# Sixty-feature groups for kv and M in a gated attention and MLP kernel, with M's last rows sent through HBM

## The chip, the cores and the metric

The kernel runs on one core of a Trainium2 chip. The time is device microseconds of one execution. The five engines are TensorE (PE, with its weight loads PEld), VectorE (DVE), ScalarE (ACT), GpSimd (POOL) and SyncE (SP, here a queue that only issues DMAs).

## What is computed

Two branches on the same 2048 tokens of 640 features, mixed by a gate. Branch A is linear attention with 32 heads of 20 features, branch B an MLP with token shifts.

```python
# A, H = 32 heads, Dh = 20
pq, pk = phi(q), phi(k)                      # phi(t) = where(t>0, t+1, exp(t)) + 1e-6
kv  = einsum("bhsd,bhse->bhde", pk, v)       # 20x20 for each head
z   = einsum("bhsd->bhd", pk)
num = einsum("bhqd,bhde->bhqe", pq, kv)
den = einsum("bhqd,bhd->bhq", pq, z)[..., None] + 1e-6
a   = (num / den) @ wo
# B
h   = gelu(layernorm(x) @ w1)                # its four quarters shifted by +1, -1, +2, -2 tokens
x1  = x + shifted(h) @ w2
b   = x1 + gelu(layernorm(x1) @ w3) @ w4
out = g * a + (1 - g) * b                    # g = sigmoid(sum(x * gate_w))
```

## The kernel before

Everything is kept in SBUF in bf16 and summed in PSUM, which has eight banks of 512 fp32 columns. The work comes in this order: q and k of each of 16 token tiles (128 tokens), with phi on ACT and DVE; G = x^T pk, gathered over the tokens in PSUM (`gr_step`, `gt_step`); then w1 and w2 of branch B, w3, and a long stretch in which `a_tile` and `w4_tile` alternate for the 16 token tiles and write the output. Because v = x wv, kv is computed from G: kv = wv^T G.

The part around the change:

- `kvt_group` (L950, its matmuls L964) makes the transposed kv in blocks of 120 features (six heads; R6 = 120). For each of six blocks, the last of 40, five matmuls with a 128x128 weight tile. The first call does four blocks, the second two.
- `lt_evac` (L968) multiplies each block by a mask that keeps the 20x20 diagonal pieces and writes it as `Lt`, on DVE (L643).
- `m_group(r)` (L981) multiplies a block of `Lt` by the matching rows of wo (`wo_aug`): M = kv wo, one matmul of 512 columns and one of 128 (L613), evacuated on ACT (L669). Blocks 0 to 4 go to rows 0 to 119 of `M_sb[:, r, :]`. Block 5 has the last 40 features, which go to `Mt`.
- `m_tail` (L991) copies the 40 rows of `Mt` by five DMAs, eight rows each, to rows 120 to 127 of the five tiles of `M_sb`, so that M lies in five full tiles of 128 rows.
- `qn_scale` (L1065) divides phi(q) by the denominator and writes it in the same order of features, a main part (L1077) and a tail; `qt_tile` (L1080) transposes it by a DMA on SP into `pqnT`.
- `a_tile` (L1085) multiplies `pqnT` by `M_sb`; its first matmuls are the first to read `M_sb`.

Other lines: L613 is the helper of nearly all matmul groups; L1050 is `w3_half`, which uses the array as two halves of 64 columns; L1115 and L1118 are `w4_half`, which uses it as two halves of 64 rows; L1136 is w4; L669 and L668 are ACT operations; L635, L643, L650 and L652 are elementwise operations on DVE or POOL; L286 is any DMA copy, L282 any DMA transpose.

Order. Each piece of work is an item with a stream, a duration and dependencies (`IT.add`). A planner (`_Items.run`) picks, item by item, the one that can start first by its own cost figures, and so fixes at build time the order of instructions on each engine. At run time every engine, the SP queue too, goes through its list strictly in order and waits on semaphores. PSUM banks are chosen by the planner as well: `bank()` and `pair()` take the bank, or the aligned pair, that comes free first, and a bank in `bank_hold` is not given away.

Before, SP's list around the change is: transposes of `xn` up to number 7, five copies of `m_tail`, transposes 8 to 11, the first six transposes of q, transposes 12 to 15, then q's other transposes.

Of the kernel before, what the change touches and what calls it, by code (L numbers as in the profile page):

```python
# [19 lines left out]
EPS_LN = 1e-5  # L20
EPS_PHI = 1e-6
NK = D + 4
R6 = 120

SB_LO = 16512
SB_HI = 229344
# [403 lines left out]
def _build(nc, A_x, A_wqkv, A_wo, B_w1, B_w2, B_w3, B_w4, gate_w, out, dbg=None, stop=None):  # L430
# [47 lines left out]

    ones_c = pa.alloc("ones_c", [128, 768], BF16)
    ident = pa.alloc("ident", [128, 128], BF16)  # L480
    mask = pa.alloc("mask120", [128, 6, 20], BF16)
    mask_t = pa.alloc("mask_t", [128, 6, 20], BF16)
# [188 lines left out]
    def memset(engf, ap, val):  # L671
        return engf(lambda e: e.memset(ap, val), [], [ap])
# [54 lines left out]
    def load_wvo():  # L727
        dp = [k_done[11]]
        sch.dma("pool", wv[:, :, :], A_wqkv[:, 2 * D:3 * D].rearrange("(k p) f -> p k f", p=128), "wv", deps=dp)
        for r in range(6):  # L730
            n = min(R6, D - R6 * r)
            sch.dma("pool", wo_aug[0:n, r, :], A_wo[R6 * r:R6 * r + n, :], "wo", group_total=6, deps=dp)

    memset(pool, ones_c[:], 1.0)
    aselect(ident[:], ones_c[:, 0:128], [[-1, 128]], ALU.is_equal, 0, 1)
    memset(pool, negh[:], -0.5)
    aselect(mask_t[0:120], ones_c[0:120, 0:120].rearrange("p (b d) -> p b d", b=6), [[-20, 6], [0, 20]], ALU.is_ge, 0, 1)
    aselect(mask[0:120], mask_t[0:120], [[20, 6], [0, 20]], ALU.is_ge, 19, -1)
# [209 lines left out]
    kv_bank = {}  # L948

    def kvt_group(h):  # L950
        b = pair()
        kv_bank[h] = b
        bank_hold.update((b, b + 1))
        mms = []
        for q_, r in enumerate(range(4) if h == 0 else range(4, 6)):
            n = min(R6, D - R6 * r)
            for k in range(KD):
                mms.append((ps[:, b, R6 * q_:R6 * q_ + n], wvf[:, D * k + R6 * r:D * k + R6 * r + 128], GT[:, k, R6 * r:R6 * r + n],
                            q_ == 0 and k == 0, k == KD - 1))

        def fn(e):
            ins = None
            for o, l, r_, st_, sp_ in mms:
                ins = e.matmul(o, l, r_, start=st_, stop=sp_, skip_group_check=True)  # L964
            return ins
        pe(fn, [wvf[:, :], GT[:, :, :]], [ps[:, b, 0:480], ps[:, b + 1, 0:1]], cost=len(mms) * 60.0)

    def lt_evac(h):  # L968
        b = kv_bank[h]
        for q_, r in enumerate(range(4) if h == 0 else range(4, 6)):  # L970
            n = min(R6, D - R6 * r)
            src = ps[0:n, b, R6 * q_:R6 * q_ + n].rearrange("p (h m i) -> p h m i", m=5, i=4)
            msk = mask[0:n, 0:n // DH, :].rearrange("p h (m i) -> p h m i", i=4)
            if r < 5:
                dst = Lt[0:n, r, 0:n].rearrange("p (h m i) -> p h m i", m=5, i=4)
            else:
                dst = Lt[0:n, r, 0:n].rearrange("p (m h i) -> p h m i", m=5, i=4)
            tt(dve, dst, src, msk, ALU.mult)
        bank_hold.difference_update((b, b + 1))

    def m_group(r):  # L981
        n = min(R6, D - R6 * r)
        kr = R6 if r < 5 else 128
        b = pair()
        mm_group(ps[:, b, 0:512], [(Lt[0:kr, r, :], wo_aug[0:kr, r, 0:512])])
        mm_group(ps[:, b + 1, 0:128], [(Lt[0:kr, r, :], wo_aug[0:kr, r, 512:D])])
        src = psf[0:n, 512 * b:512 * b + D]
        dst = M_sb[0:n, r, :] if r < 5 else Mt[0:n, :]
        activation(dst, src, ACTF.Copy)

    def m_tail():  # L991
# [9 lines left out]
    for h in range(2):  # L1001
        IT.add("KVF", ("kvt", h), 0.0, lambda h=h: kvt_group(h), deps=[(("g", KD - 1), 1.0), (("gr",), 2.5)])
        IT.add("KVF", ("lt", h), 0.0, lambda h=h: lt_evac(h), deps=[(("kvt", h), 0.0)])
# [61 lines left out]
    def qn_scale(t):  # L1065
        sd = qn_slot[t]
        ts(dve, dnr[:, 0, sd, :], dnr[:, 0, sd, :], EPS_PHI, None, ALU.add, ALU.bypass)
        dve(lambda e: e.reciprocal(dnr[:, 1, sd, :], dnr[:, 0, sd, :]), [dnr[:, 0, sd, :]], [dnr[:, 1, sd, :]], cost=350.0)
        blk = pq_tok[:, t, :].rearrange("p (j c) -> p j c", c=128)
        main = (blk[:, :, 0:R6].rearrange("p j (a d) -> p j a d", d=DH),  # L1070
                pq_tok[:, t + 1, 0:5 * R6].rearrange("p (j a d) -> p j a d", a=6, d=DH),
                dnr[:, 1, sd, 0:30].rearrange("p (j a) -> p j a", a=6).unsqueeze(3).to_broadcast([128, 5, 6, DH]), 850.0)
        tail = (blk[:, :, R6:128].rearrange("p m (h i) -> p h m i", i=4),
                pq_tok[:, t + 1, 5 * R6:D].rearrange("p (h m i) -> p h m i", h=2, i=4),
                dnr[:, 1, sd, 30:32].unsqueeze(2).unsqueeze(3).to_broadcast([128, 2, 5, 4]), 150.0)
# [218 lines left out]
```

## Time and profile before

| | |
|---|---|
| median of 3 runs | 263.45 us (263.12 to 265.74) |
| the profiled execution, whole time | 262.97 us |
| its span | 260.9 us |
| busy: PE, PEld, DVE, ACT, POOL | 257.1, 133.0, 149.1, 107.2, 97.3 us |
| share of PE in the chain that ended last | 97% |
| matmuls of kvt (L964) | 30, start 77.0 to 79.5 us |
| matmuls of `m_group` | 12, start 114.7 to 137.6 us |
| copies of `m_tail` on SP | 5, start 118.3 to 121.3 us |
| first matmul that reads `M_sb` | 139.8 us |

A matmul's duration in the profile counts its whole way through the array, and matmuls overlap; so the time that a group takes is read from the start of its first matmul to the start of the next group's. A view of one engine's timeline gives start, length, engine, line, operation and count, and in brackets how long the engine had been idle and what released it. In the rows of groups stand the busy time, the mean of one in ns, and the idle time before them.

### The profile page before, as it was taken

What the parts mean: (1) busy time and instruction counts of PE and PEld (TensorE: products, weight loads), DVE (VectorE), ACT (ScalarE), POOL (GpSimd) and SP (SyncE); (2) the same over time, 40 slices, a digit from 0 to 9 for tenths busy, and PEclk for the clock granted to TensorE, in tenths of its full rate; (3) what the DMA queues carried; (4) which work ended last, traced back from release to release, by engine and by line L of the source; (5) the groups of instructions that cost most, each with busy time, mean ns of one, the idle gap of its engine ahead of it and who ended that gap; (6) DMA issues with size and microseconds to landing.
All of it is one profiled execution on the core that took longest, in us unless ns stands there. A gap on an engine that the chain in (4) does not pass through costs nothing.

```text
span 260.9 us, 4205 instructions
## 1 busy us (share of the span) xinstructions
PE 257.1 (99%) x1651; PEld 133.0 (51%) x1651; DVE 149.1 (57%) x267; ACT 107.2 (41%) x216; POOL 97.3 (37%) x150
## 2 busy tenths in 40 slices
PE   8999999999999999999999999999999999999996
PEld 3555555544455555555444545554455544455553
DVE  2497887899903799979993407991033410143333
ACT  1396677751365757674974240005500045100000
POOL 5013995859964017958763202320011200011000
PEclk9999999999999999999999999999999999999999
DMA  7755999652766991363585610232000020000211
GB/s 205 247 90 139 171 206 156 172 108 50 102 126 126 333 353 36 71 78 59 102 125 111 122 25 0 47 92 65 0 3 0 0 103 0 0 3 0 101 53 50
DMA packets 51283, 24.98 MB, mean 96 GB/s; under 512 B 42644, under 2 KB 49853, under 8 KB 51264
## 3 DMA queue, kind: packets, MB, share of 16 engines
q1 hardware_dynamic: 49824, 21.15, 36.8%
q0 software_dynamic: 1152, 3.28, 5.4%
q8 instruction: 13, 0.21, 0.3%
q10 hardware_dynamic: 288, 0.30, 0.3%
q14 instruction: 6, 0.05, 0.1%
HBM read 12.04 MB, written 2.62 MB: 56 GB/s over the span
## 4 chain that ended last, share of the span: by engine, by line
PE 97%; DMA 1%; DVE 1%; issue 0%
PE ps L613 61%; PE ps L1136 21%; PE ps L811 7%; PE ps L887 2%; PE ps L791 1%; DMA x_tok<-in_A_x_dram 1%; PE ps L1050 1%; PE ps L1118 1%; DVE x_tok L652 1%; PE ps L964 1%; PE ps L888 1%; PE ps L624 0%; PE ps L792 0%; DVE xT L678 0%; PE ps L1115 0%
## 5 line engine op out<-in xcount | busy, mean ns | idle before, releaser
L613 PE MATMUL ps<-xnT,w 128*128 128x512 bf16 x360 | 82.3, 379 | 0.0
L1136 PE MATMUL ps<-w,h2T 128*128 128x512 bf16 (+1 forms) x416 | 58.8, 299 | 0.0
L669 ACT ACTIVATE h2T<-ps 128x512 bf16<-128x512 f32 x52 | 30.4, 598 | 66.5 <-PE ps L613 66.5
L613 PEld LDWEIGHTS ps<-xnT,w 128*128 128x128 bf16 x360 | 34.0, 98 | 37.4 <-issue 0.4
L652 DVE SCALAR_TENSOR_TENSOR x_tok<-ps,stg,abx 128x512 bf16<-128x512 f32 (+1 forms) x32 | 17.2, 550 | 61.6 <-PE ps L1136 61.6
L635 POOL TENSOR_SCALAR abx<-x_tok,stg 128x640 f32<-128x640 bf16 x16 | 14.8, 928 | 99.6 <-DVE x_tok L652 95.1
L1136 PEld LDWEIGHTS ps<-w,h2T 128*128 128x128 bf16 x416 | 32.4, 98 | 25.6 <-issue 1.1
L635 POOL TENSOR_SCALAR xn<-x_tok,st 128x640 bf16<-128x640 bf16 x32 | 38.9, 1222 | 14.5 <-DMA xnT<-xn 14.0
L669 ACT ACTIVATE Er<-ps 128x640 bf16<-128x640 f32 x32 | 22.4, 706 | 18.1 <-PE ps L613 8.5
L668 ACT ACTIVATE junk<-x_tok 128x640 bf16<-128x640 bf16 x32 | 23.6, 738 | 3.7 <-DVE x_tok L650 3.2
L669 ACT ACTIVATE hsT<-ps 128x512 bf16<-128x512 f32 (+1 forms) x32 | 18.9, 594 | 14.7 <-PE ps L613 14.3
L613 PE MATMUL ps<-M_sb,pqnT 128*128 128x512 bf16 (+1 forms) x160 | 24.3, 299 | 0.0
L613 PE MATMUL ps<-w,hsT 128*128 128x512 bf16 (+1 forms) x160 | 23.9, 299 | 0.0
L652 DVE SCALAR_TENSOR_TENSOR abx<-ps,stg,abx 128x640 f32<-128x640 f32 x16 | 14.1, 884 | 15.8 <-PE ps L613 15.8
L613 PE MATMUL ps<-wkg,xT 128*128 128x512 bf16 (+1 forms) x150 | 22.6, 299 | 0.0
L613 PEld LDWEIGHTS ps<-w,hsT 128*128 128x128 bf16 x160 | 13.3, 98 | 12.3
L613 PEld LDWEIGHTS ps<-M_sb,pqnT 128*128 128x128 bf16 x160 | 13.1, 98 | 10.4
L613 PE MATMUL ps<-wq,xT 128*128 128x512 bf16 (+1 forms) x120 | 18.3, 299 | 0.0
L811 PE MATMUL ps<-pk_tok,x_tok 128*128 128x512 bf16 x80 | 17.8, 379 | 0.0
L650 DVE SCALAR_TENSOR_TENSOR x_tok<-ps,x_tok 128x640 bf16<-128x640 f32 x16 | 13.1, 821 | 6.9 <-PE ps L613 6.0
L635 DVE TENSOR_SCALAR Er<-Er 128x640 bf16<-128x640 bf16 x32 | 11.8, 369 | 8.6 <-ACT Er L669 8.3
L613 PEld LDWEIGHTS ps<-wkg,xT 128*128 128x128 bf16 x150 | 12.1, 97 | 9.0
(74 smaller groups left out, 236.2 us busy)
## 6 DMA issues: line engine op xcount, KB each, us to landing
w<-in_B_w_dram SPq DMA_DIRECT2D x1, 2160.0 KB, 8.2
w<-in_B_w_dram SPq DMA_DIRECT2D x1, 2080.0 KB, 14.9
x_tok<-in_A_x_dram SPq DMA_DIRECT2D x3, 640.0 KB, 5.9
out_dram<-x_tok SPq DMA_DIRECT2D x3, 640.0 KB, 3.2
w<-in_B_w_dram POOLq DMA_DIRECT2D x8, 160.0 KB, 4.8
wkg<-in_A_wqkv_dram SPq DMA_DIRECT2D x5, 160.0 KB, 4.3
wv<-in_A_wqkv_dram POOLq DMA_DIRECT2D x1, 800.0 KB, 6.4
wo_aug<-in_A_wo_dram POOLq DMA_DIRECT2D x5, 150.0 KB, 5.2
```

What stands on the lines that cost most here:

```text
L613: ins = e.matmul(out_ap, l, r, start=(i == 0), stop=(i == n - 1))
L635: return engf(lambda e: e.tensor_scalar(out_ap, in_ap, s1, s2, op0, op1), rd, [out_ap], cost=cost)
L650: return dve(lambda e: e.scalar_tensor_tensor(out_ap, in0, scalar, in1, op0, op1, accum_out=accum), rd, [out_ap, accum], cost=cost + 70.0)
L652: return dve(lambda e: e.scalar_tensor_tensor(out_ap, in0, scalar, in1, op0, op1), rd, [out_ap], cost=cost)
L668: return act(lambda e: e.activation(out_ap, in_ap, func, bias=bias, scale=scale, accum_out=accum), rd, wr, cost=cost)
L669: return act(lambda e: e.activation(out_ap, in_ap, func, bias=bias, scale=scale), rd, wr, cost=cost)
L791: e.matmul(ps[:, b, :], l, x_tok[:, t, 0:512], start=(t == 0), stop=(t == NT - 1))
L811: ins = e.matmul(ps[:, b, :], l, r, start=(t0 + q_ == 0), stop=(t0 + q_ == NT - 1))
L887: e.matmul(ps[:, b, 0:512], l, w[:, k, 0:512], start=(k == 0), stop=(k == KD - 1))
L888: return e.matmul(ps[:, b + 1, 0:n2], l, w[:, k, 512:512 + n2], start=(k == 0), stop=(k == KD - 1))
L964: ins = e.matmul(o, l, r_, start=st_, stop=sp_, skip_group_check=True)
L1136: ins = e.matmul(o, l, r, start=False, stop=(i == KFF - 1), skip_group_check=(n0 > 0))
```

## The change

kv is made in blocks of 60 features (three heads; R3 = 60) instead of 120. Two blocks lie side by side in the partitions of PSUM, at 0 to 59 and 64 to 123, each from a weight tile of 64 columns, so that a pair of matmuls uses the two column halves of the array. There are 50 matmuls of 60 columns and five of 40, in one bank and one call. The masks are four DVE operations instead of six.

Of M, blocks 0 to 7 are made by `m_quads`: 16 matmuls on 64x64 quarters of the array into six banks held together, evacuated by six ACT operations. Blocks 8 and 9 are one `m_group(4)` of 128 rows, the last 40 features `m_group(5)` as before. M's tiles now have 60 + 4 rows twice, so the 40 rows of `Mt` go to partitions 60 to 63 and 124 to 127. They are written to a scratch tensor in HBM by one DMA (`m_send`) and loaded from there by two (`m_tail`). The items are due after the w3 groups 0, 3 and 6 of the first chunk, instead of after every third group.

As built, the planner puts the quads behind the eighth w3 group (number 7) and `m_group(4)` behind the ninth; `m_group(5)` moves one w2 tile ahead. The first matmul that reads `M_sb` stands behind as many w3 groups as before. SP's list becomes: transposes of `xn` up to number 7, the store of `m_send`, transposes 8 to 11, the first six transposes of q, transposes 12 to 14, the two loads of `m_tail`, transpose 15, then q's other transposes. On POOL `wo_aug` is cleared whole at the start, and wo is loaded by seven DMAs instead of six.

```diff
-R6 = 120
+R3 = 60
+PAIRS = ((0, 2), (1, 3), (4, 6), (5, 7), (8, 9), (10,))
...
-        for r in range(6):
-            n = min(R6, D - R6 * r)
-            sch.dma("pool", wo_aug[0:n, r, :], A_wo[R6 * r:R6 * r + n, :], "wo", group_total=6, deps=dp)
+        for c, r, g, m in ((0, 0, 0, 2), (1, 0, 2, 2), (0, 2, 4, 2), (1, 2, 6, 2), (0, 4, 8, 1), (1, 4, 9, 1)):
+            sch.dma("pool", wo_aug[64 * c:64 * c + R3, r:r + m, :],
+                    A_wo[R3 * g:R3 * (g + m), :].rearrange("(g p) d -> p g d", p=R3), "wo", group_total=7, deps=dp)
+        sch.dma("pool", wo_aug[0:D - 10 * R3, 5, :], A_wo[10 * R3:D, :], "wo", group_total=7, deps=dp)
...
-    memset(pool, wo_aug[:, 5, :], 0.0)
+    memset(pool, wo_aug[:], 0.0)
...
+    def kvt_group():
+        b = bank()
...
+        for r, gs in enumerate(PAIRS):
             for k in range(KD):
+                for c, g in enumerate(gs):
+                    n = min(R3, D - R3 * g)
+                    mms.append((ps[64 * c:64 * c + 64, b, R3 * r:R3 * r + n], wvf[:, D * k + R3 * g:D * k + R3 * g + 64],
+                                GT[:, k, R3 * g:R3 * g + n], r == 0 and k == 0, k == KD - 1))
...
+    def m_quads():
+        held = [bank() for _ in range(6)]
+        bs, bt = held[:4], held[4:]
+        bank_hold.update(held)
...
+        for i in range(2):
+            jobs = []
+            for h in range(2):
+                rows = slice(64 * h, 64 * h + 64)
+                for c in range(2):
+                    jobs.append((ps[64 * c:64 * c + 64, bs[2 * i + h], :], Lt[rows, 2 * i + c, 0:64],
+                                 wo_aug[rows, 2 * i + c, 0:512], True))
+            quad(jobs, [ps[:, bs[2 * i + h], :] for h in range(2)])
...
+        for j in range(4):
+            activation(M_sb[:, j, 0:512], ps[:, bs[j], :], ACTF.Copy)
+        for h in range(2):
+            activation(M_sb[:, h:4:2, 512:D], ps[:, bt[h], 0:256].rearrange("p (i n) -> p i n", n=128), ACTF.Copy)
+        bank_hold.difference_update(held)
+
+    m_rows = nc.dram_tensor("m_rows", [D - 10 * R3, D], BF16, kind="Internal").ap()
+    m_sent = []
+
+    def m_send():
+        m_sent.append(sch.dma("sp", m_rows, Mt[0:D - 10 * R3, :], "ms"))
+
     def m_tail():
-        for j in range(KD):
-            sch.dma("sp", M_sb[R6:128, j, :], Mt[8 * j:8 * j + 8, :], "mt", group_total=KD)
+        src = m_rows.rearrange("(j c p) d -> c p j d", c=2, p=4)
+        for c in range(2):
+            p0 = 64 * c + R3
+            sch.dma("sp", M_sb[p0:p0 + 4, :, :], src[c], "mt", group_total=2, deps=m_sent)
...
-    for n, r in enumerate((5, 0, 1, 2, 3, 4)):
-        IT.add("KVF", ("m", r), 0.0, lambda r=r: m_group(r), deps=[(("lt", 1), 1.0), (("w3", (1 + 3 * n) // KFF, (1 + 3 * n) % KFF), 0.0)])
-    IT.add("MT", ("mt",), 0.0, m_tail, deps=[(("m", 5), 1.5), (("t1", NT - 1), 0.0)])
+    IT.add("KVF", ("m", 5), 0.0, lambda: m_group(5), deps=[(("lt",), 1.0), (("w3", 0, 0), 0.0)])
+    IT.add("MT", ("ms",), 0.0, m_send, deps=[(("m", 5), 1.5)])
+    IT.add("KVF", ("mq",), 0.0, m_quads, deps=[(("w3", 0, 3), 0.0)])
+    IT.add("KVF", ("m", 4), 0.0, lambda: m_group(4), deps=[(("w3", 0, 6), 0.0)])
+    IT.add("MT", ("mt",), 0.0, m_tail, deps=[(("m", 4), 1.0), (("t1", NT - 1), 0.0)])
```

More of the change, by code (lines that the diff above doesn't have):

```diff
@@ L480, in _build @@
     ident = pa.alloc("ident", [128, 128], BF16)
-    mask = pa.alloc("mask120", [128, 6, 20], BF16)
-    mask_t = pa.alloc("mask_t", [128, 6, 20], BF16)
+    mask = pa.alloc("mask60", [128, R3], BF16)
+    mask_t = pa.alloc("mask_t", [128, 3, R3], BF16)
     negh = pa.alloc("negh", [128, 4], F32)
@@ L946, in _build @@
     IT.add("MISC", ("gr",), 0.0, gr_turn, deps=[(("g0", NT - 1), 1.0)])
[L948 to L953, printed above, removed]
+    kv_bank = []
+    def kvt_group():
+        b = bank()
+        kv_bank.append(b)
+        bank_hold.add(b)
         mms = []
-        for q_, r in enumerate(range(4) if h == 0 else range(4, 6)):
-            n = min(R6, D - R6 * r)
+        for r, gs in enumerate(PAIRS):
             for k in range(KD):
-                mms.append((ps[:, b, R6 * q_:R6 * q_ + n], wvf[:, D * k + R6 * r:D * k + R6 * r + 128], GT[:, k, R6 * r:R6 * r + n],
-                            q_ == 0 and k == 0, k == KD - 1))
+                for c, g in enumerate(gs):
+                    n = min(R3, D - R3 * g)
+                    mms.append((ps[64 * c:64 * c + 64, b, R3 * r:R3 * r + n], wvf[:, D * k + R3 * g:D * k + R3 * g + 64],
+                                GT[:, k, R3 * g:R3 * g + n], r == 0 and k == 0, k == KD - 1))
         def fn(e):
@@ L965, in fn @@
             return ins
[L966 to L979, printed above, removed]
+        pe(fn, [wvf[:, :], GT[:, :, :]], [ps[:, b, 0:6 * R3]], cost=1100.0)
@@ new lines, in lt_evac @@
+    def lt_evac():
+        b = kv_bank[0]
+        n = D - 10 * R3
+        tt(dve, Lt[0:n, 5, 0:n], ps[0:n, b, 5 * R3:5 * R3 + n], mask[0:n, 0:n], ALU.mult)
+        tt(dve, Lt[:, 0:4, 0:R3], ps[:, b, 0:4 * R3].rearrange("p (r d) -> p r d", d=R3),
+           mask[:, :].unsqueeze(1).to_broadcast([128, 4, R3]), ALU.mult)
+        for c in range(2):
+            rows = slice(64 * c, 64 * c + 64)
+            tt(dve, Lt[rows, 4, 64 * c:64 * c + R3], ps[rows, b, 4 * R3:5 * R3], mask[rows, :], ALU.mult)
+        bank_hold.discard(b)
@@ L981, in m_group @@
     def m_group(r):
-        n = min(R6, D - R6 * r)
-        kr = R6 if r < 5 else 128
         b = pair()
-        mm_group(ps[:, b, 0:512], [(Lt[0:kr, r, :], wo_aug[0:kr, r, 0:512])])
-        mm_group(ps[:, b + 1, 0:128], [(Lt[0:kr, r, :], wo_aug[0:kr, r, 512:D])])
+        mm_group(ps[:, b, 0:512], [(Lt[:, r, :], wo_aug[:, r, 0:512])])
+        mm_group(ps[:, b + 1, 0:128], [(Lt[:, r, :], wo_aug[:, r, 512:D])])
+        n = 128 if r < 5 else D - 10 * R3
         src = psf[0:n, 512 * b:512 * b + D]
-        dst = M_sb[0:n, r, :] if r < 5 else Mt[0:n, :]
+        dst = M_sb[:, 4, :] if r < 5 else Mt[0:n, :]
@@ L989, in m_group, with quad, fn @@
         activation(dst, src, ACTF.Copy)
+    def m_quads():
+        held = [bank() for _ in range(6)]
+        bs, bt = held[:4], held[4:]
+        bank_hold.update(held)
+        def quad(jobs, aps):
+            def fn(e):
+                ins = None
+                for o, l, r_, st_ in jobs:
+                    ins = e.matmul(o, l, r_, start=st_, stop=True, skip_group_check=True)
+                return ins
+            pe(fn, [Lt[:, 0:4, 0:64], wo_aug[:, 0:4, :]], aps, cost=len(jobs) / 4 * nfree(jobs[0][0]) * 0.4167 + 100.0)
+        for i in range(2):
+            jobs = []
+            for h in range(2):
+                rows = slice(64 * h, 64 * h + 64)
+                for c in range(2):
+                    jobs.append((ps[64 * c:64 * c + 64, bs[2 * i + h], :], Lt[rows, 2 * i + c, 0:64],
+                                 wo_aug[rows, 2 * i + c, 0:512], True))
+            quad(jobs, [ps[:, bs[2 * i + h], :] for h in range(2)])
+        jobs = []
+        for i in range(2):
+            for h in range(2):
+                rows = slice(64 * h, 64 * h + 64)
+                for c in range(2):
+                    jobs.append((ps[64 * c:64 * c + 64, bt[h], 128 * i:128 * (i + 1)], Lt[rows, 2 * i + c, 0:64],
+                                 wo_aug[rows, 2 * i + c, 512:D], i == 0))
+        quad(jobs, [ps[:, bt[h], 0:256] for h in range(2)])
+        for j in range(4):
+            activation(M_sb[:, j, 0:512], ps[:, bs[j], :], ACTF.Copy)
+        for h in range(2):
+            activation(M_sb[:, h:4:2, 512:D], ps[:, bt[h], 0:256].rearrange("p (i n) -> p i n", n=128), ACTF.Copy)
+        bank_hold.difference_update(held)
@@ L999, in zb_group @@
         copy(dve, zb[:, :], psf[:, 512 * b:512 * b + D])
-    for h in range(2):
-        IT.add("KVF", ("kvt", h), 0.0, lambda h=h: kvt_group(h), deps=[(("g", KD - 1), 1.0), (("gr",), 2.5)])
-        IT.add("KVF", ("lt", h), 0.0, lambda h=h: lt_evac(h), deps=[(("kvt", h), 0.0)])
-    for n, r in enumerate((5, 0, 1, 2, 3, 4)):
-        IT.add("KVF", ("m", r), 0.0, lambda r=r: m_group(r), deps=[(("lt", 1), 1.0), (("w3", (1 + 3 * n) // KFF, (1 + 3 * n) % KFF), 0.0)])
-    IT.add("MT", ("mt",), 0.0, m_tail, deps=[(("m", 5), 1.5), (("t1", NT - 1), 0.0)])
+    IT.add("KVF", ("kvt",), 0.0, kvt_group, deps=[(("g", KD - 1), 1.0), (("gr",), 2.5)])
+    IT.add("KVF", ("lt",), 0.0, lt_evac, deps=[(("kvt",), 0.0)])
+    IT.add("KVF", ("m", 5), 0.0, lambda: m_group(5), deps=[(("lt",), 1.0), (("w3", 0, 0), 0.0)])
[3 more added lines that the diff above has]
+    IT.add("MT", ("mt",), 0.0, m_tail, deps=[(("m", 4), 1.0), (("t1", NT - 1), 0.0)])
     IT.add("ZB", ("zb",), 0.0, zb_group, deps=[(("z", NT - 1), 1.7), (("w2", 0), 0.0)])
@@ L1068, in qn_scale @@
         dve(lambda e: e.reciprocal(dnr[:, 1, sd, :], dnr[:, 0, sd, :]), [dnr[:, 0, sd, :]], [dnr[:, 1, sd, :]], cost=350.0)
[L1069 to L1074, printed above, removed]
+        blk = pq_tok[:, t, :].rearrange("p (s c) -> p s c", c=64)
+        main = (blk[:, :, 0:R3].rearrange("p s (a d) -> p s a d", d=DH),
+                pq_tok[:, t + 1, 0:10 * R3].rearrange("p (s a d) -> p s a d", a=3, d=DH),
+                dnr[:, 1, sd, 0:30].rearrange("p (s a) -> p s a", a=3).unsqueeze(3).to_broadcast([128, 10, 3, DH]), 850.0)
+        tail = (blk[:, :, R3:64].rearrange("p (h m) i -> p h m i", m=5),
+                pq_tok[:, t + 1, 10 * R3:D].rearrange("p (h m i) -> p h m i", h=2, i=4),
                 dnr[:, 1, sd, 30:32].unsqueeze(2).unsqueeze(3).to_broadcast([128, 2, 5, 4]), 150.0)
@@ L1190, in _build @@
     IT.add("MISC", ("w3load",), 0.0, w3_load, deps=[(("k", NT - 1), 0.0), (("t1", NT - 1), 0.0)])
-    IT.add("MISC", ("w4load",), 0.0, w4_load, deps=[(("kvt", 1), 0.0), (("t1", NT - 1), 0.0), (("z", NT - 1), 1.5)])
+    IT.add("MISC", ("w4load",), 0.0, w4_load, deps=[(("kvt",), 0.0), (("t1", NT - 1), 0.0), (("z", NT - 1), 1.5)])
     for c in range(NCH):
@@ L1195, in _build @@
             if c == 0 and j == 0:
-                deps0 = [(("kvt", 1), 0.0), (("z", NT - 1), 1.5)]
+                deps0 = [(("kvt",), 0.0), (("z", NT - 1), 1.5)]
             else:
```

11 lines of the change are left out of this document (8 added, 3 removed).

## The prediction

> **What bounds the kernel now.** I read the page's busy times and clock row first, then the chain that ended last, then the view of who waited for whom, kept to TensorE, and last the timelines of single engines.
>
> ```profile
> PE 257.1 (99%) x1651; PEld 133.0 (51%) x1651; DVE 149.1 (57%) x267; ACT 107.2 (41%) x216; POOL 97.3 (37%) x150
> PEclk9999999999999999999999999999999999999999
> PE 97%; DMA 1%; DVE 1%; issue 0%
> PE ps L860 <- PEq L1279: 0.8, 1, 0.8
> ```
>
> TensorE is busy 257.1 of 260.9 us, it is 97% of the chain, and the waits view lists a single wait for it, 0.8 us at the start. So a microsecond of TensorE work saved is worth a microsecond, and every new wait of TensorE is paid in full. The change must be judged as TensorE time plus TensorE waits; what DVE, ACT, POOL and SP do counts only where TensorE ends up waiting.
>
> **kvt.** TensorE's timeline around it, the one existing use of the two column halves (w3_half, L1050), and the weight loads of both:
>
> ```profile
> 76.96 1.21 PE L964 MATMUL ps<-GT,wv 128*128 128x120 bf16 x20
> 78.01 1.24 PE L613 MATMUL ps<-xnT,w 128*128 128x512 bf16 x5
> 79.09 0.55 PE L964 MATMUL ps<-GT,wv 128*128 128x120 bf16 x10
> 79.48 2.32 PE L613 MATMUL ps<-xnT,w 128*128 128x512 bf16 x10
> 149.66 2.35 PE L1050 MATMUL ps<-xnT,w 128*64 128x512 bf16 x20
> 151.94 2.33 PE L613 MATMUL ps<-xnT,w 128*128 128x512 bf16 x10
> L964 PEld LDWEIGHTS ps<-GT,wv 128*128 128x128 bf16 x30 | 1.7, 98 | 0.5 <-issue 0.2
> L1050 PEld LDWEIGHTS ps<-xnT,w 128*64 128x64 bf16 x20 | 1.0, 110 | 1.2 <-issue 0.4
> ```
>
> Read from start to start: 78.01-76.96 = 1.05 us for 20 matmuls of 120 columns (52.5 ns each), and 79.48-79.09 = 0.39 us for five of 120 and five of 40, so (0.39-0.26)/5 = 25.5 ns for one of 40. Removed: 1.44 us. Five 512-column matmuls take 79.09-78.01 = 1.08, 216 ns each. The 20 of w3_half take 151.94-149.66 = 2.28: ten pairs at 216 ns and 0.12 us over, so the halves do overlap, and entering and leaving costs about 0.12. Added: 55 matmuls of 60 or 40 columns, in pairs. Low bound: pairs overlap completely, 55 x 25.5 / 2 = 0.70. High bound: each waits for its own 110 ns load, 6.05. I take the issue pace, since the 40-column row is the nearest: 55 x 25.5 ns + 0.12 = 1.52, that is +0.1 us (bounds -0.7 and +4.6).
>
> [...]
>
> **M.**
>
> ```profile
> 119.02 7.72 PE L613 MATMUL ps<-xnT,w 128*128 128x512 bf16 x35
> 126.57 0.44 PE L613 MATMUL ps<-wo_aug,Lt 120*128 120x512 bf16 x2
> 126.85 1.24 PE L613 MATMUL ps<-xnT,w 128*128 128x512 bf16 x5
> 137.39 0.44 PE L613 MATMUL ps<-wo_aug,Lt 120*128 120x512 bf16 x2
> 139.82 1.52 PE L613 MATMUL ps<-M_sb,pqnT 128*128 128x512 bf16 x10
> 154.21 0.39 PE L1118 MATMUL ps<-w,h2h 64*128 64x512 bf16 x2
> 154.86 1.47 PE L1136 MATMUL ps<-w,h2T 128*128 128x512 bf16 x6
> ```
>
> One m_group costs 126.85-126.57 = 0.28 us (0.216 + 0.056). m5 and m4 stay; four groups, 1.09 us, become eight 512-column and eight 128-column matmuls on four quarter arrays: 2 x 0.216 + 2 x 0.056 = 0.54. w4_half, two row halves at a time, takes 154.86-154.21 = 0.65 where 0.54 is ideal, so 0.11 for the switch. That is -0.43 us (bounds: only two at a time +0.1; no switch cost -0.54).
>
> **Waits for PSUM banks.** m_quads takes six banks at once, and its six evacuations go to ACT in one block behind the GELUs. ACT there, now:
>
> ```profile
> 123.83 0.74 ACT L668 ACTIVATE junk<-x_tok 128x640 bf16<-128x640 bf16 x1 [1.30 <-DVE x_tok L650]
> 124.56 3.02 ACT L669 ACTIVATE h2T<-ps 128x512 bf16<-128x512 f32 x6
> 127.43 0.74 ACT L669 ACTIVATE M_sb<-ps 120x640 bf16<-120x640 f32 x1
> ```
>
> ACT is late here: it waits for DVE until 123.83 and then does six GELUs back to back, some 0.5 us apart, the first of them for w3 group 3, up to 127.4. The quads come after group 7, at 119.02 + 6 x 1.08 = 125.5. In the built order their tails wait for the GELU of group 5 (done about 126.1, 0.2 us late), group 8 for that of group 6 (126.6, 0.4 late), and m4 for the second and third new evacuation (about 128.1 and 128.6, together 0.6 late). Some 1.2 us of new waits (bounds 0.5 and 2), and behind them on TensorE stands everything else. TensorE then reaches the first tile of a_tile at 139.82 + 0.1 - 0.43 + 1.2 = 140.7.
>
> **M's last rows.** That tile also waits for m_tail. SP issues strictly in order:
>
> ```profile
> 117.11 1.20 SPq L282 DMA_TRANSPOSE xnT<-xn  x1
> 118.35 3.55 SPq L286 DMA_DIRECT2D M_sb<-Mt  x5
> 121.94 5.98 SPq L282 DMA_TRANSPOSE xnT<-xn  x4
> 127.96 8.29 SPq L282 DMA_TRANSPOSE pqnT<-pq_tok  x6
> 139.41 2.55 SPq L282 DMA_TRANSPOSE xnT<-xn  x2
> L286 SPq DMA_DIRECT2D M_sb<-Mt x5: 624/663/776, 118.3 to 121.3; - x5
> 119.84 3.81 POOL L635 TENSOR_SCALAR xn<-x_tok,st 128x640 bf16<-128x640 bf16 x3
> 125.33 1.36 POOL L635 TENSOR_SCALAR xn<-x_tok,st 128x640 bf16<-128x640 bf16 x1 [1.68 <-DMA xnT<-xn]
> ```
>
> Now the five copies leave at 118.35, 21 us before they are needed. In the changed order only the store (ms) stands there. The two loads (mt) stand behind four xnT, six pqnT and three more xnT transposes, ahead of the last xnT, because they need m4's evacuation. That evacuation, at about 131, is not what holds them: SP is. A transpose occupies SP 1.2 to 1.3 us, and the queue is full to 142. How much earlier does it run? The store replaces five issues of 0.66, ending at 119.0; the next transpose then waits for POOL's first xn, 119.84 + 3.81/3 = 121.1, instead of 121.94: 0.8 us sooner. The fourth waits for POOL, which waits for the first to land, so all shift by the same 0.8. The 15th xnT, now at 139.41, goes at 138.6; mt at 139.9 and, 0.7 later, 140.6.
>
> ```profile
> wq<-in_A_wqkv_dram ACTq DMA_DIRECT2D x1, 160.0 KB, 3.0
> out_dram<-x_tok SPq DMA_DIRECT2D x1, 32.0 KB, 1.6
> M_sb<-Mt SPq DMA_DIRECT2D x5, 10.0 KB
> ```
>
> The present copies show no landing time. The load is 25 KB: between the 1.6 us of a 32 KB store and the 3.0 of a 160 KB load from HBM; I take 2.0, near the one of its size. mt lands at 142.6, 142.7 with kvt's 0.1, and the tile starts about 0.1 later, 142.8, against 139.82: +3.0 us. The earlier PSUM waits and the 0.43 saved are swallowed, because TensorE stands until 142.8 anyway. TensorE works in order, so everything behind (w3 groups, w4 tiles) moves by the same 3.0, and nothing later has room to give it back. Behind mt on SP stand the last xnT and nine pqnT; their readers are TensorE's later w3 and a_tile groups, which have moved too. Bounds: if the freed SP time and a quicker POOL step advance the queue by 1.6 and the load takes 1.6, 139.1 + 0.7 + 1.6 = 141.4, +1.6; with no advance and 3.0, 140.7 + 0.7 + 3.0 = 144.4, +4.6.
>
> **What costs nothing.**
>
> ```profile
> L672 POOL MEMSET wo_aug<- 128x640 bf16 x1 | 0.6, 632 | 0.0
> L635 POOL TENSOR_SCALAR st<-lr 128x4 f32<-128x4 f32 x4 | 1.0, 248 | 19.0 <-ACT lr L669 19.0
> L286 POOL DMA_DIRECT2D wo_aug<-in_A_wo_dram x6 | 3.2, 539 | 0.0
> ```
>
> POOL's wo_aug memset grows sixfold, from 0.63 to about 3.8 us, with some masks; POOL then idles for ACT's lr, 19.0 us in three waits. One more wo load (0.54 on POOL) lies in such a wait too. Lt's masks on DVE go from six to four operations, q's scaling keeps its element counts, and m5, one w2 tile sooner, only changes places with it. If POOL's cover were gone, the cost would be the 3.2 us of the longer memset.
>
> **Sum.** The profiled execution took 262.97 us (span 260.9 and 2.1 around it), 0.2% under the median of 263.45. 262.97 + 3.0 = 266.0.
>
> **Rivals.**
> 1. Not slower: the loads land before TensorE arrives and ACT's late GELUs clear in time, so that only TensorE's work changes: +0.1 - 0.43, 262.6. It decides if mt lands before 139.5, 3.1 us ahead of my working; the full SP queue speaks against it. With banks alone waited for, 262.97 + 0.9 = 263.9; for it, that ACT's lateness is in the trace.
> 2. kvt's loads are exposed. If a load and a matmul take turns, each at the 25.5 ns of the 40-column pair, kvt takes 55 x 51 ns + 0.12 = 2.9 us, 1.4 more than in the sum: 267.4; at 110 ns each, 4.5 more: 270.5. It decides from the point where loads no longer hide under 25 ns matmuls. Against it: L1050 hid them, but under long matmuls.
> 3. The clock falls during the 2.1 us (140.7 to 142.8) in which TensorE stands still.
>
> ```profile
> L860 PE MATMUL ps<-const-bfloat16-1.0 128*128 128x512 bf16 x6 | 2.7, 626 | 0.8 <-PEq L1279 0.8
> L613 PE MATMUL ps<-xnT,w 128*128 128x512 bf16 x360 | 82.3, 379 | 0.0
> ```
>
> The six opening matmuls took 2.7/6 = 0.45 us each against 0.216 later: half pace. A slow stretch as long as those six, 2.7 us, costs 1.4: 267.4. Against it: no wait like this is in the trace, and the row of the clock is full throughout. [...]
>
> **Chances.** Forecast 0.70, rival 1 0.05, banks alone 0.08, rival 2 0.08, rival 3 0.09. Low end: banks alone, 263.9; high end: rivals 2 and 3 at their nearer prices, 268.0. A measurement of this kernel can tell about 1% from no change, here 2.6 us. Faster by that would need more than kvt's bound and the quads' together: 0.02. Slower: rivals 2 and 3 and two thirds of the forecast (mt more than 2.6 late), 0.63. Within: 0.35.
>
> **What would show it.** Right: in the profile after, one wait of TensorE of about 2 us, by the DMA that writes M_sb, just before the first M_sb matmul near 142.8; SP's two M_sb loads near 140, behind pqnT transposes; 55 matmuls of kvt in about 1.5 us; short waits for ACT near 126 to 129. Wrong: M_sb loads that land before 140.5, a kvt stretch over 2.5 us, or a clock row under 9 near 143.

## Result and the profile after

The changed kernel takes 264.74 us (median of 22 runs, 264.22 to 265.93) against 263.40 for the kernel before (22 runs): ratio 1.0049, 95% interval 1.0038 to 1.0060. It is slower, as forecast, but by 1.3 us (0.5%) where 266.0 had been forecast, 2.6 over the median of before and 3.0 over its profiled run. The profiled execution took 264.64 us, 1.67 more than the profiled one before. Where a run's mean granted clock is below 1.000, it is given beside its time, and the ratios of the two sets with both edits below leave out one such run each (266.44 and 266.77 us, both at 0.994).

The page of the changed kernel, busy times, clock and chain:

```profile
PE 257.4 (98%) x1684; PEld 132.1 (50%) x1684; DVE 149.2 (57%) x265; ACT 107.0 (41%) x218; POOL 100.5 (38%) x154
PEclk9999999999999999999999999999999999999999
PE 90%; DVE 5%; ACT 2%; DMA 1%; issue 0%; SPq 0%; DVEq 0%
```

TensorE still bounds the kernel, and its clock row is full, but its share of the chain fell from 97% to 90%: DVE and ACT are now on it. The waits view shows where TensorE meets them, and that the loads of M's last rows are met as well, by a weight load (PEld):

```profile
PE ps L1005 <- ACT h2T L670: 0.8, 2, 0.6
PE ps L614 <- ACT M_sb L670: 0.2, 1, 0.2
PE ps L614 <- ACT h2T L670: 0.2, 1, 0.2
PEld ps L614 <- DMA M_sb<-m_rows: 0.5, 1, 0.5
```

There is no wait of 2 us for the DMA. TensorE's timeline around the three edits (L972 kvt, L1005 the quads, M_sb the first `a_tile`):

```profile
76.03 1.24 PE L614 MATMUL ps<-xnT,w 128*128 128x512 bf16 x5
77.20 1.13 PE L972 MATMUL ps<-GT,wv 128*64 128x60 bf16 x55
78.26 1.90 PE L614 MATMUL ps<-xnT,w 128*128 128x512 bf16 x8
...
118.90 6.64 PE L614 MATMUL ps<-xnT,w 128*128 128x512 bf16 x30
125.46 0.41 PE L1005 MATMUL ps<-wo_aug,Lt 64*64 64x512 bf16 x4
126.10 0.41 PE L1005 MATMUL ps<-wo_aug,Lt 64*64 64x512 bf16 x4 [0.23 <-ACT h2T L670]
127.08 0.31 PE L1005 MATMUL ps<-wo_aug,Lt 64*64 64x128 bf16 x8 [0.56 <-ACT h2T L670]
127.56 1.25 PE L614 MATMUL ps<-xnT,w 128*128 128x512 bf16 x5 [0.18 <-ACT h2T L670]
129.03 0.72 PE L614 MATMUL ps<-wo_aug,Lt 128*128 128x512 bf16 x2 [0.21 <-ACT M_sb L670]
129.58 12.03 PE L614 MATMUL ps<-xnT,w 128*128 128x512 bf16 x55
141.63 1.53 PE L614 MATMUL ps<-M_sb,pqnT 128*128 128x512 bf16 x10
```

kvt takes 78.26 - 77.20 = 1.06 us. Between the end of w3 group 7 (118.90 + 30 x 0.216 = 125.38) and 129.58 lie 4.20 us, far more than the work in them (0.68 of quads, 1.08 of w3, 0.28 of `m4`, so 2.16 too much). The waits view counts only 1.2 of that, because it takes a matmul as busy for its whole length in the profile (379 ns on average for one of 512 columns, while they follow each other every 216); read from start to start, the stall is the whole 2.16. From 129.58, eleven w3 groups of 1.08 us bring TensorE to 141.46. The first `M_sb` matmul starts at 141.63, 1.81 later than before (139.82), only 0.17 after TensorE could have come there. So two things end almost together: TensorE's own arrival, made late by ACT, and the landing of the loads. The same stretch on the other engines:

```profile
119.03 2.60 POOL L636 TENSOR_SCALAR xn<-x_tok,st 128x640 bf16<-128x640 bf16 x3
114.14 0.48 DVE L636 TENSOR_SCALAR dnr<-dnr 128x32 f32<-128x32 f32 x1
120.06 0.75 DVE L636 TENSOR_SCALAR dnr<-dnr 128x32 f32<-128x32 f32 x1
124.74 0.74 ACT L669 ACTIVATE junk<-x_tok 128x640 bf16<-128x640 bf16 x1 [2.33 <-DVE x_tok L651]
125.47 2.52 ACT L670 ACTIVATE h2T<-ps 128x512 bf16<-128x512 f32 x5
119.94 5.17 SPq L283 DMA_TRANSPOSE xnT<-xn  x4
138.50 0.76 SPq L287 DMA_DIRECT2D M_sb<-m_rows  x2
```

ACT's block of GELUs starts at 125.47, 0.9 later than before (124.56); the two loads leave SP from 138.50, behind transposes that run ahead of what had been reckoned.

### The profile page after: what moved, and what is told of

It reads as the page before. It is cut to its first block, busy times and chain, and to the rows that moved or that the text cites. A ratio compares the mean times of both kernels' runs of the same rounds, so it can differ in the third digit from the quotient of the medians.

```text
span 262.7 us, 4275 instructions
## 1 busy us (share of the span) xinstructions
PE 257.4 (98%) x1684; PEld 132.1 (50%) x1684; DVE 149.2 (57%) x265; ACT 107.0 (41%) x218; POOL 100.5 (38%) x154
## 4 chain that ended last, share of the span: by engine, by line
PE 90%; DVE 5%; ACT 2%; DMA 1%; issue 0%; SPq 0%; DVEq 0%
PE ps L614 56%; PE ps L1185 21%; PE ps L818 7%; PE ps L894 2%; DVE x_tok L651 2%; DMA x_tok<-in_A_x_dram 1%; PE ps L798 1%; ACT h2T L670 1%; PE ps L1099 1%; PE ps L1167 1%; DVE pq_tok L1126 1%; DVE x_tok L653 1%; DVE dnr L1109 1%; DVE qprod L644 1%; ACT M_sb L670 1%; PE ps L895 0%
## 5 line engine op out<-in xcount | busy, mean ns | idle before, releaser
L636 POOL TENSOR_SCALAR abx<-x_tok,stg 128x640 f32<-128x640 bf16 x16 | 14.8, 924 | 104.1 <-DVE x_tok L653 95.1
L636 POOL TENSOR_SCALAR xn<-x_tok,st 128x640 bf16<-128x640 bf16 x32 | 36.3, 1142 | 11.1 <-DMA xnT<-xn 10.6
L636 DVE TENSOR_SCALAR Er<-Er 128x640 bf16<-128x640 bf16 x32 | 11.3, 353 | 9.0 <-ACT Er L670 8.6
```

Source lines behind the costliest of these rows:

```text
L636: return engf(lambda e: e.tensor_scalar(out_ap, in_ap, s1, s2, op0, op1), rd, [out_ap], cost=cost)
```

## The experiments

The theory after this profile: **two walls** near 141.5, one made by the quads that wait on ACT's late GELUs, the other by the loads behind SP's transposes. Taking away one alone should gain nothing. The rivals are that one of them alone sets the time.

**Late quads.** Only the places of the quads and of `m4` among the w3 groups change:

```diff
-    IT.add("KVF", ("mq",), 0.0, m_quads, deps=[(("w3", 0, 3), 0.0)])
-    IT.add("KVF", ("m", 4), 0.0, lambda: m_group(4), deps=[(("w3", 0, 6), 0.0)])
+    IT.add("KVF", ("mq",), 0.0, m_quads, deps=[(("w3", 0, 10), 0.0)])
+    IT.add("KVF", ("m", 4), 0.0, lambda: m_group(4), deps=[(("w3", 0, 12), 0.0)])
```

> The quads are placed behind the twelfth w3 group (number 11) instead of the eighth, m4 behind the seventeenth, so that ACT has caught up and no PSUM bank is waited for; the loads of M's last rows stay where they are on SP. Theory A (two walls: in the changed kernel TensorE reached the first M_sb matmul at about 141.45 us because of PSUM waits, and the loads landed at about 141.6, so taking one wall away shows the other): TensorE arrives near 139.4 and waits some 2 us for the loads; the time stays at 264.7, within 0.3. Theory B (only the PSUM waits decide; the loads are hidden anyway): 2.1 us less, 262.6. Theory C (only the loads decide, as the prediction said): 264.7, with a wait of TensorE on the loads.

Measured: median 266.42 of 10 runs, ratio 1.0093 [1.0064, 1.0121], which none of the three theories gave. The runs are in two groups: four at clock 1.000, 264.2 to 265.2 (mean 264.73); six at 0.994, 266.3 to 267.0. A profiled execution of the first group, TensorE and SP:

```profile
130.11 0.74 PE L1005 MATMUL ps<-wo_aug,Lt 64*64 64x512 bf16 x16
141.39 1.53 PE L614 MATMUL ps<-M_sb,pqnT 128*128 128x512 bf16 x10 [1.54 <-DMA M_sb<-m_rows]
138.35 0.76 SPq L287 DMA_DIRECT2D M_sb<-m_rows  x2
```

The quads run in one piece, the waits for ACT are gone but for 0.16 us, and the place of the first `M_sb` matmul stays: a wait of 1.54 us for the loads has taken theirs. That is the loads' wall, and the theory that ACT's waits alone decide falls. Whether the six runs at the lower clock come from that pause is taken up below.

**Early loads.** The loads leave SP ahead of the last four `xnT` transposes (12 to 15) instead of one. Two expectations below call these "the last three"; they are four:

```diff
-        IT.add("T2", ("t2", u), 0.0, lambda u=u: t_xn(2, u), deps=[(("n2", u), 1.1)])
+        IT.add("T2", ("t2", u), 0.0, lambda u=u: t_xn(2, u), deps=[(("n2", u), 1.1)] + ([(("mt",), 0.0)] if u == 12 else []))
```

> The two loads of M's last rows are put on SP ahead of the transposes of xn 12 to 14 (three transposes sooner, about 4 us); the quads stay where they are. Theory A (two walls 0.15 us apart): 264.6, 0.1 to 0.2 less than the changed kernel, no wait on the loads, all PSUM waits still there. Theory B (PSUM waits alone): 264.7, no change. Theory C (the loads alone; PSUM waits of 1.2 us as predicted): TensorE would start M_sb at 140.7, 0.9 less: 263.8.

Measured: 264.62 (12 runs), 1.0047 [1.0031, 1.0064]. TensorE's waits and the two ends:

```profile
PE ps L1005 <- ACT h2T L670: 0.8, 2, 0.6
PE ps L614 <- ACT M_sb L670: 0.7, 1, 0.7
133.97 0.74 SPq L287 DMA_DIRECT2D M_sb<-m_rows  x2
141.11 1.52 PE L614 MATMUL ps<-M_sb,pqnT 128*128 128x512 bf16 x10
```

The loads leave 4.5 us sooner and nobody waits for them; the time does not move. That is ACT's wall, and the theory that the loads alone decide (263.8) falls.

**Both** edits together, run twice:

> Both edits together: quads behind the twelfth w3 group and the loads ahead of the transposes of xn 12 to 14. Theory A: both walls are gone, what is left is TensorE's own work, kvt 0.3 to 0.4 us shorter and the quads 0.54 + 0.1 instead of 1.09: first M_sb matmul near 139.1, time 0.7 to 0.9 us below the kernel before, 262.6. Theory B: 262.6 as well, and equal to the run with late quads alone. Theory C: as with early loads alone, 263.8, or less by the PSUM waits.

> Late quads and loads ahead of the last three xnT once more, the same kernel as in the first call, beside the version with kvt alone. Theory: 262.8 again, ratio about 0.9975, no wait for the loads, 0.2 us for ACT. Rival (the gain of 0.25% was chance): 263.3, ratio 1.000.

Measured: 262.82 (12 runs), 0.9975 [0.9956, 0.9993], and again 262.58 (9 runs), 0.9969 [0.9956, 0.9982]: faster than both kernels. The second one, TensorE, then ACT:

```profile
130.00 0.74 PE L1005 MATMUL ps<-wo_aug,Lt 64*64 64x512 bf16 x16
130.68 4.49 PE L614 MATMUL ps<-xnT,w 128*128 128x512 bf16 x20
139.59 1.52 PE L614 MATMUL ps<-M_sb,pqnT 128*128 128x512 bf16 x10
125.72 3.99 ACT L670 ACTIVATE h2T<-ps 128x512 bf16<-128x512 f32 x8
```

ACT's GELUs are as late as ever; by 130 it has done eight of them, and the quads' six evacuations no longer stand in the way of a w3 group. The quads cost 130.68 - 130.00 = 0.68 us, switch included. Without either wall the change gains 0.1 to 0.4% by the two intervals, 0.2 to 1.2 us. The work that it saves on TensorE, 0.3 for kvt and 0.3 for the quads by the rows below, lies in the middle of that. The loads leave only from 136.42 here, because they need `m4`, 3.2 us ahead of the first `M_sb` matmul, so the two ends stay close.

**Why ACT is late.** DVE adds 1e-6 to the denominators (L636), once for each token tile. The addition at 120.06 took 0.75 us and the one at 114.14 took 0.48, where the kernel before took 0.18 for each, and each ended within 0.05 us of the end of a POOL `xn` operation. The one of before beside the second, which began 0.04 us after an `xn` operation (119.84):

```profile
119.88 0.18 DVE L635 TENSOR_SCALAR dnr<-dnr 128x32 f32<-128x32 f32 x1
```

Two kernels leave all these additions out, one with early loads and one without; all other instructions keep their places:

```diff
-        ts(dve, dnr[:, 0, sd, :], dnr[:, 0, sd, :], EPS_PHI, None, ALU.add, ALU.bypass)
-        dve(lambda e: e.reciprocal(dnr[:, 1, sd, :], dnr[:, 0, sd, :]), [dnr[:, 0, sd, :]], [dnr[:, 1, sd, :]], cost=350.0)
+        dve(lambda e: e.reciprocal(dnr[:, 1, sd, :], dnr[:, 0, sd, :]), [dnr[:, 0, sd, :]], [dnr[:, 1, sd, :]], cost=350.0 + 138.3)
```

With early loads:

> As the run with early loads, and without the small DVE operation that adds 1e-6 to the denominators (128x32 fp32; left out of the computation). The order of all other work is the same. In the changed kernel this operation took 0.75 us at 120.06 instead of 0.18, ending when an operation of POOL ended, and made the last w2 evacuation, ACT's square and its GELU block 0.9 us late. Theory D (DVE stood still for POOL there, and that made the PSUM waits longer than predicted): the GELU block starts 0.7 to 0.9 us sooner, and the time falls by as much against the run with early loads: 263.8. Rival (the lateness comes from DVE's work itself, not from POOL): only the 0.2 us of the operation are saved: 264.4.

Measured: 263.40 (12 runs), 0.9996 [0.9982, 1.0010], 1.2 us under early loads alone, more than the 0.7 to 0.9 expected. The removal takes away the work of the additions as well as their delay, so it shows that these additions make ACT late, not how much of it is POOL's doing. Its POOL, ACT and TensorE:

```profile
118.78 3.80 POOL L636 TENSOR_SCALAR xn<-x_tok,st 128x640 bf16<-128x640 bf16 x3
124.36 2.52 ACT L670 ACTIVATE h2T<-ps 128x512 bf16<-128x512 f32 x5
140.34 1.52 PE L614 MATMUL ps<-M_sb,pqnT 128*128 128x512 bf16 x10
```

With the loads where the change put them:

> The changed kernel with its quads and its loads where they are, without the DVE operation that adds 1e-6 to the denominators (left out of the computation); no other instruction changes its place. Theory (two walls of nearly the same place: late GELUs on ACT, and the loads behind the transposes on SP): without the 0.75 us operation the GELUs start 0.8 earlier, TensorE comes to the first M_sb matmul at about 140.4, but the loads still land near 141.4, so a wait of about 1 us for the loads takes the place of the waits for ACT and the time stays at 264.5 (where the loads went earlier the same removal brought 1.2). Rival (only ACT's lateness sets the time in the changed kernel): 263.4, as with the earlier loads, and no wait for the loads.

Measured: 264.65 (12 runs), 1.0031 [1.0010, 1.0052]. TensorE:

```profile
125.56 0.74 PE L1005 MATMUL ps<-wo_aug,Lt 64*64 64x512 bf16 x16
141.70 1.53 PE L614 MATMUL ps<-M_sb,pqnT 128*128 128x512 bf16 x10 [1.38 <-DMA M_sb<-m_rows]
```

The same removal is worth 1.2 us where the loads are early. Where they are not, the medians differ by 0.1 us and the intervals of the two ratios overlap (1.0031 [1.0010, 1.0052] and 1.0049 [1.0038, 1.0060]): 1.4 us of waiting for the loads appear in place of ACT's. The rival that ACT alone sets the time (263.4) falls again, as the rival of the loads alone fell with early loads.

**kvt alone.** kvt in column halves as in the change, but M as six plain groups, five of them due behind every second w3 group (as built behind the groups 8, 9, 10, 12 and 13), and early loads. The masks, in three DVE operations, and the loads of wo, three, are not printed here:

```diff
-PAIRS = ((0, 2), (1, 3), (4, 6), (5, 7), (8, 9), (10,))
+PAIRS = ((0, 1), (2, 3), (4, 5), (6, 7), (8, 9), (10,))
...
-    IT.add("KVF", ("mq",), 0.0, m_quads, deps=[(("w3", 0, 3), 0.0)])
-    IT.add("KVF", ("m", 4), 0.0, lambda: m_group(4), deps=[(("w3", 0, 6), 0.0)])
+    for n, r in enumerate((0, 1, 2, 3, 4)):
+        IT.add("KVF", ("m", r), 0.0, lambda r=r: m_group(r), deps=[(("w3", 0, 4 + 2 * n), 0.0)])
```

> kvt in column halves as in the changed kernel, but M's 64x64 products again as six plain groups of two products of 128 rows, spread over the w3 groups as in the kernel before; M's last rows through the scratch, loads ahead of the last three xnT. Theory (kvt saves 0.3, the quads in groups save 0.4, and only the block of six evacuations behind the late GELUs costs): kvt stretch 1.06 us at 78, no wait of TensorE for ACT or for the loads, and a time of 262.97 - 0.3 = 262.7, some 0.3 over the version with late quads. Rival (kvt's gain comes back somewhere, and the gain of the version with late quads is all from the quads): 263.0 to 263.3, no different from before. If the six evacuations one by one also meet the late GELUs: 263.5.

Measured: 263.07 (12 runs), 0.9989 [0.9979, 0.9999], a gain of 0.03 to 0.55 us. kvt takes 1.06 us again, and although the GELUs come as late after the start of w3 (119.37 here) as in the changed kernel, no group waits for them:

```profile
77.67 1.13 PE L972 MATMUL ps<-GT,wv 128*64 128x60 bf16 x55
78.73 3.41 PE L614 MATMUL ps<-xnT,w 128*128 128x512 bf16 x15
125.94 3.01 ACT L670 ACTIVATE h2T<-ps 128x512 bf16<-128x512 f32 x6
```

So the late GELUs by themselves cost nothing; it is the block that takes six banks at once, with its six evacuations, that TensorE meets. The median lies in the range of the rival (263.0 to 263.3), and the interval is too wide to tell the gain of 0.3 from a smaller one. The trace still has it: from the start of kvt to the first `M_sb` matmul 62.48 us (77.67 to 140.15), against 62.86 before.

**A longer pause.** Late quads, and the loads behind one transpose more:

```diff
-    IT.add("MT", ("mt",), 0.0, m_tail, deps=[(("m", 4), 1.0), (("t1", NT - 1), 0.0)])
+    IT.add("MT", ("mt",), 0.0, m_tail, deps=[(("m", 4), 1.0), (("t1", NT - 1), 0.0), (("t2", NT - 1), 0.0)])
```

> Late quads as before, and the two loads of M's last rows one xnT transpose later on SP (1.25 us). Theory (TensorE's clock falls when it stands some 1.5 us or more, and then runs a few us at a lower pace): the loads leave near 139.6, the first M_sb matmul at about 142.6 after a wait of 2.8 us; every run shows a mean clock of 0.994, the page a clock digit under 9 near 143, w3 and M_sb matmuls there take over 400 ns instead of 216, and the time is 264.4 + 1.2 + 1.6 to 2.2 = 267.4. Rival (the lower clock in six of ten runs with late quads has nothing to do with the wait): clock 1.0 in part of the runs again, 265.6 where it is 1.0, and matmuls at 216 ns right behind the wait.

Measured: six runs, 265.4 at clock 1.000, three of 266.7 to 267.2 at 0.993 to 0.994, two of 269.3 at 0.987; median 267.23, ratio 1.016 [1.0118, 1.0201]. "Every run" was too much: one run stayed at 1.000 and took 265.4, as the rival had it. The rest held in the profiled run. TensorE in the profiled one (266.69), and the view by stretches of time (busy, count, granted clock, DMA share, GB/s):

```profile
142.30 2.85 PE L614 MATMUL ps<-M_sb,pqnT 128*128 128x512 bf16 x10 [2.55 <-DMA M_sb<-m_rows]
144.94 1.37 PE L614 MATMUL ps<-xnT,w 128*128 128x512 bf16 x5
146.15 1.52 PE L614 MATMUL ps<-M_sb,pqnT 128*128 128x512 bf16 x10
141.00:141.50 0.50, 0.00 (x0) 1.00 0.30 82
141.50:142.00 0.50, 0.00 (x0) 0.78 1.13 208
142.00:142.50 0.50, 0.20 (x1) 0.50 0.54 91
145.00:145.50 0.50, 0.50 (x4) 0.81 0.29 57
```

TensorE stands from 142.30 - 2.55 = 139.75 on. The clock falls to half near 141.8, still in the pause, and rises near 145.2. The ten matmuls take 144.94 - 142.30 = 2.64 us instead of 1.36 and the next five 1.21 instead of 1.08: 1.4 us lost, beyond the wait. Runs at 0.987 were 3.9 us over the one at 1.000, runs at 0.993 to 0.994 1.3 to 1.8, so they probably fell twice; no trace shows the second fall.

**Both kernels once more**, for their profiles:

> The kernel before once more, for its profile. Theory (the fifth xnT transpose landed late in the first profile by chance or by its code's place, and this made SP's queue look later than it is in the changed kernel): if by chance, POOL's fourth xn starts near 113.8 instead of 115.5 after a wait near 1.0 us, the copies of m_tail leave 1.5 us earlier or SP's transposes after them start before 121; if it belongs to this kernel, 115.5 and a wait of 2.6 us again, transposes from 121.9. 263.0 either way.

> The changed kernel once more, for its profile. Theory (its order decides, not chance): DVE's addition to the denominators at 120 takes 0.75 us again, GELUs from 125.5, loads leave SP at 138.4 to 138.6, first M_sb matmul near 141.6, 264.7. Rival (the phase of DVE and POOL is chance): 0.18 us for that operation, GELUs from 124.6, a wait for the loads of about 1 us, the same time.

Measured: before 267.73, after 265.17 (one run each). The run of before had a pause of its own, 2.7 us at 42 us for the transposed x, and a lower clock after it (mean 0.994), so its time is not compared and its rows are 4.5 to 4.8 us late. Its POOL and SP, then DVE, ACT, SP and TensorE of the changed kernel:

```profile
120.01 1.86 POOL L635 TENSOR_SCALAR xn<-x_tok,st 128x640 bf16<-128x640 bf16 x1 [2.37 <-DMA xnT<-xn]
126.68 5.87 SPq L282 DMA_TRANSPOSE xnT<-xn  x4
```

```profile
120.24 0.77 DVE L636 TENSOR_SCALAR dnr<-dnr 128x32 f32<-128x32 f32 x1
125.67 2.53 ACT L670 ACTIVATE h2T<-ps 128x512 bf16<-128x512 f32 x5
138.75 0.76 SPq L287 DMA_DIRECT2D M_sb<-m_rows  x2
142.17 1.53 PE L614 MATMUL ps<-M_sb,pqnT 128*128 128x512 bf16 x10 [0.35 <-DMA M_sb<-m_rows]
```

Both patterns come back: the late landing in both profiles of the kernel before, the long addition in both of the changed one. So chance is an unlikely reason for either. The first `M_sb` matmul came 0.5 later than expected, with a wait of 0.35 us for the loads: in this run the landing ends last more plainly than in the first.

## Why the prediction was right and wrong, point by point

**Direction and place: right.** The loss is where it was put, between w3 group 7 and the first `M_sb` matmul, everything behind it moved along, and the rest of the kernel gave almost nothing back (1.81 us at that matmul, 1.67 at the end). By the 1% that the prediction itself drew as its line, a loss of 0.5% is "within", to which it had given 0.35, and not "slower" (0.63). Of its signs, the short waits for ACT and the loads behind pqnT transposes came; the wait of 2 us for the DMA and a kvt of 1.5 us did not. Its high end of 268.0 does not follow from its rivals: each alone gives 267.4, both together 268.8.

**The step that failed: the landing of the loads, and with it the pause.** Forecast was a landing at 142.7 and the tile at 142.8, +3.0 us, with TensorE standing for the last 2.1 of them; measured is the tile at 141.63, +1.8, with TensorE standing 0.17. Transpose 8 was to wait for POOL's first `xn` until 121.1; it left at 119.94. The error was to take POOL's times from the kernel before. There POOL's fourth `xn` had waited 2.65 us for a landing and began at 115.50; in the changed kernel:

```profile
113.71 0.88 POOL L636 TENSOR_SCALAR xn<-x_tok,st 128x640 bf16<-128x640 bf16 x1 [0.99 <-DMA xnT<-xn]
```

POOL therefore began its next three at 119.03 instead of 119.84, and took 0.87 us each, where before one of the three had taken 2.08. That put transpose 8 1.2 sooner than forecast, and the queue gained 0.2 more on its way, so the first load left 1.4 sooner (138.50, not 139.9). The second follows 0.4 later, not 0.7. Together 1.7 sooner. Against that, the loads take longer: from the issue of the second to the matmul that waits for it 141.70 - 139.0 = 2.7 us where the additions are left out and 2.6 with late quads, where 2.0 was taken (bounds 1.6 to 3.0). The sooner issue outweighs the longer load. The lower end given for this term, +1.6, was the near one.

**The waits for ACT: right mechanism, wrong size, and not swallowed.** They came to 2.2 us, where 1.2 (0.5 to 2) had been forecast, just over its bound. From the start of w3, ACT's block came 1.03 us later than before (125.47 - 118.90 against 124.56 - 119.02). The additions lost 0.30 and 0.57 of that beside POOL's `xn`, the operation after the second one (L1126) 0.15. So TensorE came at 141.46, not 140.7, and the waits that the loads were to swallow became a wall of their own. POOL's sooner start, 113.71 instead of 115.50, seems to lie behind both errors: it freed the queue, and by these rows it set POOL's operations beside DVE's additions; no run moved it alone. That the two errors brought the walls together to 0.17 us is luck. With a TensorE at 140.7 the loads would still have held it to about 141.6, as without the additions, where it could have come at 128.29 + 55 x 0.216 = 140.17 and started at 141.70.

**kvt: a small gain, not a small loss.** +0.1 forecast, 1.06 for the matmuls and 0.09 for the entry against 1.44: -0.3. The pace is 19 ns a matmul, under the 25.5 ns I had taken as the pace of issue; pairs in the two halves overlap in part. Rival 2 (exposed loads) is wrong by the row of kvt's weight loads in the changed kernel:

```profile
L972 PEld LDWEIGHTS ps<-GT,wv x55: 107/112/113, 77.2 to 78.1; 128*64 128x64 bf16 x55
```

55 loads of 112 ns fit into one microsecond, so they overlap each other too. Each is slower than a load of kvt before (112 ns for 64 columns, 98 for 128), but no such load sets the pace: the matmuls follow each other every 19 ns.

**Quads: right.** In the second version with both edits, 0.68 and 0.08 for the entry (130.00 against 119.12 + 50 x 0.216 = 129.92, where w3 starts at 119.12) against 1.09: -0.33, forecast -0.43.

**Rival 1** (not slower, 262.6) is what the version with both edits does (262.82 and 262.58). Both its conditions, loads that land in time and GELUs out of the way, had to be made by moving the loads and the quads. Its number was partly luck, since its sum has +0.1 for kvt, which is -0.3, and the rows' sum of -0.6 came out as 0.5 and 0.7 us under the medians of before in the same two sets (263.29 and 263.24).

**Rival 3** (the clock falls in the pause) did not happen in the changed kernel, whose waits after the start are 0.6 us at most in its first profile and whose 22 runs all kept a clock of 0.999 or more. With a pause of 2.55 us it happened in five of six runs, and the trace shows 1.41 us lost, the price that the prediction gave. With late quads six of ten runs had a lower clock and were 1.9 us longer; the one trace, with a pause of 1.54 us, is of a run at 1.000. The version without the additions waits 1.38 us for the same loads, and none of its twelve runs fell. So a pause near 1.5 us may cost this, but only the clock of those six runs, not a trace, ties them to it. Single runs at 0.994 also came from kernels whose profiles have no pause at these copies or loads: one in each set with both edits, which has no trace, and the run of before above, whose trace has a pause at 42 us. In the longer pause TensorE stood from 139.75 and the clock fell near 141.8, some 2 us later; why it falls in some runs of one kernel and not in others, no run shows. For the pause of 2.1 us that was forecast, a chance of 0.09 looks too low.

**Cover.** The longer memset, the masks and the additional wo load cost nothing that shows: the version with both edits is faster by about what kvt and the quads save, so by that estimate no more than some tenths of a microsecond can be hidden there.

**Open.** Why the fifth transpose lands late in the kernel before is not settled. The ten profiles of kernels with the scratch show 1.0 us there, both of before 2.4 to 2.7; no run took one part of it away.

## What to carry to other kernels

When a change adds a wait, look for the second one that ends near it: gain and loss of each alone can be nothing, and only the pair of experiments (take away one, the other, both) shows it. Times of engines that feed a queue are not constants to carry from the trace of before; give a queue's advance a range of a microsecond or two wherever an edit frees it. Spread what must pass a late engine instead of sending it in one block. Count a pause of TensorE as a risk to its clock as well: one of 2.55 us cost 1.4 more here, and with one of 1.54 us six of ten runs had a lower clock, while with one of 1.38 us none of twelve had.

## What the runs showed of the hardware

- A 128x32 addition on DVE took 0.75 us instead of 0.18 when it began while POOL ran an `xn` operation, and ended within 0.05 us of its end; another took 0.48. With the additions gone, POOL's three `xn` there took 3.80 us instead of 2.60. Overlap alone does not decide which engine loses: in the kernel before, an addition began 0.04 us after an `xn` operation (0.89) and took 0.18, and the next `xn` took 2.08. Why one of the two engines is held up, no run shows.
- Matmuls of 60 columns, alternating between the two column halves, followed each other every 19 ns, with a weight load of 112 ns for every one.
- TensorE's clock fell to 0.50 about 2 us into a pause of 2.55 us and came back 3.4 us later (near 141.8 and 145.2, by the mean clocks of half a microsecond each); ten matmuls in that stretch took 2.64 us instead of 1.36. In the run of before with a pause of 2.71 us (mean clock 0.994) the ten matmuls right behind the pause took 1.73 us, where ten of the same kind took 1.35 later, and the ten after them were busy for 2.83 us instead of 1.53: most of the loss came with those. So the slow stretch need not begin inside the pause.
- Loads of 25 KB from HBM on SP took 2.5 to 3.0 us, in four profiles, from the issue of the second to the matmul that waited for it; 2.0 had been taken, near the 1.6 us of a 32 KB store.
